# Reordering the last block of a convolution and MLP kernel: output products with the raw activations last, one of them by token halves

## The chip, the cores and the metric

The kernel runs on one core of one Trainium2 chip. The metric is the device time of one execution in microseconds (us), the median of several. A run counts as slow when it lies more than 1.5% above the fastest of the same kernel.

The span of the profile is about 1.7 us shorter than the time of the same execution.

The **tail** runs from the first matmul of the last block's output products to the end of the span, and a **tail time** counts from that same matmul.

## The reference, cut to what matters

```
x (8, 4096, 192), weight (8 heads, 7 taps), w_in (192, 2048), w_out (2048, 192), all float32

w   = softmax of weight over the taps
out = causal 7-tap convolution of x over the sequence, one set of taps per head of 24 channels
h   = out.reshape(32768, 192) @ w_in
g   = h * (1 / (1 + exp(-h)))          # silu
y   = g @ w_out                        # (32768, 192), what is stored
```

## The kernel before: the parts that matter here

The 32768 tokens are worked in 32 blocks of 1024. A block is first multiplied by `w_in` ("up") into `g`, then by `w_out` ("down"). Both products of a block use a scheme with seven products of halves of the matrices instead of eight. In "down" the halves are two token groups of 512 and two channel halves of 96, so the result has four slices: C11, C12, C21, C22, held as `c[0]` to `c[3]`.

The seven products lie in six accumulator banks (`acc[0]` to `acc[5]`, called slots 0 to 5). They are summed over four steps `j`. A slot holds a product of 96 rows, and in its last 32 rows a piece of another. Slots 0 and 1 multiply the raw `g`. Slots 2 to 5 need sums of `g` that VectorE makes first (`t`).

```
# the order of work, one token per step: t = a sum of g, z/y/x = ScalarE copies out of the
# accumulators, M = VectorE adds of the slots, o = turn and store a slice; "-" = of the block before
PLAN = (
    "P1.0 P1.1 -x1.0 -M4.0 | P1.2 P5.0 -M5.0 s1.1 -M7.0 | P5.1 E22.0 s1.0 -o.1 s1.2 | "
    "E22.1 P6.1 -o.2 | P6.0 P1.3 s2.1 | P6.2 P5.2 -o.3 s1.3 s2.0 | P5.3 P7.1 s2.2 | "
    # ... cut ...
    "t.30 | . | t.31 | w.0 | t.32 | . | t.33 | . | w.1 | w.2 | z1.0 w.3 | y0.0 | y1.0 | "
    ". | y2.0 M1.0 | M2.0 | M6.0 | x0.0 | M3.0 x2.0 | o.0"
)

def down(b, j):
    # ... cut: a_, forms: which product takes which weights and which of g and t ...
    sets = ((1, 2, 0), (3, 2, 1), (6, 2, 2), (7, 4, 0), (5, 4, 1))
    for i in (0, 1, 2, 4, 3, 5) if j < NJ - 1 else (0, 1, 2, 3, 5, 4):
        if j == 0:
            accs[b][i] = bank()
        for e in range(2):
            # ... four matmuls into the quarters of slot i, mm(i, q, every, lhs, q, rhs, e) ...
            yield

def merge(b, name):
    # ... cut: the copies x, y, z on ScalarE; the last of them is
    pin(nc.scalar.copy(to, acc[3 * (name[0] == "x") + k][n:P, :]))
    # ... and the adds on VectorE
    out_, u, v = {
        "M1": lambda: (c[1], c[0], acc[2][0:n, :]),
        "M2": lambda: (c[3], c[1], acc[1][0:n, :]),
        "M3": lambda: (c[2], c[1], acc[3][0:n, :]),
        "M4": lambda: (c[1], c[3], acc[4][0:n, :]),
        "M5": lambda: (c[3], c[2], acc[4][0:n, :]),
        "M6": lambda: (c[0], c[0], t["y"][0:n, :]),
        "M7": lambda: (c[2], c[2], t["x"][0:n, :]),
    }[name]()

def turn_out(b, i):
    # 32x32 transposes of slice i on VectorE, then one store per 32 channels
    pin(nc.vector.transpose(osb[0:top, i, :, :]..., cmbs[b][0][0:top, i, :]))
    for q in range(top // SQ):
        queue = (nc.sync, nc.scalar, nc.gpsimd)[q % 3] if b == NB - 1 else nc.sync
        queue.dma_start(out=out_v[2 * b + n][:, :, c : c + SQ], in_=osb[...])

for b in range(1, NB):
    run(b, plan[:NU])
    begin_down(b)
    slots = (None for j in range(NJ) for _ in down(b, j))
    for s in plan[NU:]:
        next(slots)
        run(b, [s])
run(NB, plan[:NU])           # what is left of the last block: x1 M4 M5 M7 o.1 o.2 o.3
```

In an inner block, the merges and the stores of the block before lie beside the next block's matmuls. Only the last block has no next one: its last copy, adds, transposes and stores lie open.

Of the kernel before, what the change touches and what calls it, by code (L numbers as in the profile page):

```python
# [9 lines left out]
F32 = mybir.dt.float32  # L10
I32 = mybir.dt.int32
AF = mybir.ActivationFunctionType
ALU = mybir.AluOpType
# [4 lines left out]
def kernel(  # L18
# [24 lines left out]
    nc = tc.nc  # L43
# [6 lines left out]
    P = 128  # L50
# [4 lines left out]
    TB = 512  # L55
    TT = 2 * TB
    NB = NT // TT
    NCH = DFF // P
    NM = NCH // 2
    NJ = NM // 2  # L60
    SQ = 32
    HD = D // 2
    NP = HD // SQ
# [3 lines left out]
    out_v = out.rearrange("(n k t) d -> n t k d", k=TB // SQ, t=SQ)  # L67

    const = ctx.enter_context(tc.tile_pool(name="const", bufs=1))
    xpool = ctx.enter_context(tc.tile_pool(name="xp", bufs=1))  # L70
    tpool = ctx.enter_context(tc.tile_pool(name="tp", bufs=3))
    gpool = ctx.enter_context(tc.tile_pool(name="gp", bufs=2 * NJ))
    upool = ctx.enter_context(tc.tile_pool(name="up", bufs=13))
# [29 lines left out]
    def pin(ins):  # L103
        return tc.keep_in_program_order(ins)
# [8 lines left out]
    vec = Pinned(nc.vector)  # L113

    def bank():
        return psum.tile([P, TB], F32, tag="ps", name="ps")
# [3 lines left out]
    def load(b):  # L120
# [12 lines left out]
        out=wexp.rearrange("p h k -> p (h k)"),  # L133
        in_=weight.rearrange("(o h) k -> o (h k)", o=1).to_broadcast([P, H * K]),
# [5 lines left out]
    for k in range(NK):  # L140
        nc.gpsimd.dma_start(
            out=xts[0][R:P, k, 0:pad], in_=x0[:, k, :], allow_slow_non_contiguous=True
# [116 lines left out]
    for e in range(2):  # L259
        half = hot[R * e : R * e + R]  # L260
        for sign, base in ((1, 0), (-1, grp - 1)):
            nc.gpsimd.affine_select(
                out=half,
                in_=half,
# [20 lines left out]
    for k in range(NK):  # L285
# [4 lines left out]
            op=ALU.mult,  # L290
# [96 lines left out]
    bk, us, sums, cmbs, accs = {}, {}, {}, {}, {}  # L387

    def product(b, m, name):
        d, t = dups[b], wins[b]  # L390
        e, r, s = m % 2, wr[m // 2], ws[m // 2]

        other, bn, w, v = {
            "P1": (0, "1", r[:, 0, 0, :], d[:, 0, 0, :]),
            "P6": (0, "1", r[:, 0, 1, :], t[:, 1, :]),
            "P7": (0, "1", r[:, 1, 0, :], t[:, 2, :]),
            "P4": (0, "1", r[:, 1, 1, :], t[:, 3, :]),
            "E21": (0, "1", r[:, 1, 2, :], d[:, 0, 2, :]),
            "P2": (1, "b", s[:, 0, 1, :], d[:, 0, 1, :]),
            "E11": (1, "b", s[:, 0, 2, :], d[:, 0, 2, :]),  # L400
            "P5": (1, "d", s[:, 1, 0, :], t[:, 0, :]),
            "E22": (1, "d", s[:, 1, 2, :], d[:, 1, 2, :]),
            "P3": (1, "d", s[:, 0, 0, :], d[:, 1, 1, :]),
            "E12": (1, "d", s[:, 1, 1, :], d[:, 1, 2, :]),
        }[name]
        half = e ^ other
        first = (b, m, bn) not in bk
        if first:
            bk[b, m, bn] = bank()
        pin(  # L410
            nc.tensor.matmul(  # L411
                bk[b, m, bn], rows(w, half), rows(v, half), start=first, stop=True,
                skip_group_check=True,
            )
        )
# [4 lines left out]
    def sums_h(b, name, m):  # L420


        if name[0] == "s":
            u = us[b, m, name[1]] = upool.tile([P, TB], F32, tag="u", name="u")
            copy = nc.vector.tensor_copy if name == "s2" else nc.scalar.copy
            pin(copy(u, bk[b, m, "1"]))  # L426
            return
        g = g_of(b, m, int(name[1]) - 1, int(name[2]) - 1)
        if name == "C21":
            pin(nc.scalar.activation(g, bk[b, m, "1"], AF.Silu))  # L430
        elif name[0] == "g":
            pin(nc.scalar.activation(g, g, AF.Silu))  # L432
        else:
            i, bn = {"C11": ("1", "b"), "C22": ("3", "d"), "C12": ("2", "d")}[name]
            pin(nc.vector.tensor_tensor(g, us.pop((b, m, i)), bk[b, m, bn], op=ALU.add))  # L435
# [15 lines left out]
        )[i]()  # L451
        pin(nc.vector.tensor_tensor(t[i // 2][:, i % 2, :], u, v, op=ALU.subtract))  # L452

    def down(b, j):



        if j == 0:
            accs[b] = {}
        g = [gs[b, j, a] for a in range(2)]  # L460
        w, x_ = wo[j], wx[j]

        def t(i):
            return sums[b, j][i // 2][:, i % 2, :].rearrange("p (e t) -> p e t", e=2)

        def mm(i, q, cols, lhs, c, rhs, e):
            pin(
                nc.tensor.matmul(  # L468
                    accs[b][i][SQ * q : SQ * q + SQ, cols],
                    lhs[:, e, SQ * c : SQ * c + SQ],  # L470
                    rhs[:, e, cols] if i < 5 else rhs[:, e, ts(q, TB // 4)],
                    start=j == 0 and e == 0,
                    stop=j == NJ - 1 and e == 1,
                    skip_group_check=True,
                )
            )

        a_ = [[w[:, a, :, HD * u : HD * u + HD] for a in range(2)] for u in range(2)]
        forms = {
            1: lambda: (a_[0][0], g[0][:, 0]),  # L480
            2: lambda: (a_[0][1], g[1][:, 0]),
            3: lambda: (x_[:, 2], g[1][:, 1]),
            4: lambda: (a_[1][1], t(3)),
            5: lambda: (x_[:, 0], t(0)),
            6: lambda: (x_[:, 1], t(1)),
            7: lambda: (a_[1][0], t(2)),
        }
        sets = ((1, 2, 0), (3, 2, 1), (6, 2, 2), (7, 4, 0), (5, 4, 1))
        every = slice(0, TB)

        for i in (0, 1, 2, 4, 3, 5) if j < NJ - 1 else (0, 1, 2, 3, 5, 4):
            if j == 0:
                accs[b][i] = bank()
            for e in range(2):
                if i < 5:
                    own, other, c = sets[i]
                    for q in range(NP):
                        lhs, rhs = forms[own]()
                        mm(i, q, every, lhs, q, rhs, e)
                    lhs, rhs = forms[other]()  # L500
                    mm(i, NP, every, lhs, c, rhs, e)
                else:
                    lhs, rhs = forms[4]()
                    for q in range(4):
                        mm(5, q, slice(0, TB // 4), lhs, 2, rhs, e)
                yield
        for a in range(2):
            del gs[b, j, a]
# [63 lines left out]
    osbs = {}  # L572

    def turn_out(b, i):
        if b not in osbs:
            osbs[b] = tpool.tile([P, 4, TB // SQ, SQ], F32, tag="t", name="osb")
        osb = osbs[b]
        top = HD if b else P
        pin(
            nc.vector.transpose(  # L580
                osb[0:top, i, :, :].rearrange("p k c -> p (k c)"), cmbs[b][0][0:top, i, :]
            )
        )
        for q in range(top // SQ):
            n, c = (i % 2, HD * (i // 2) + SQ * q) if b else (q // 2, R * i + SQ * (q % 2))
            queue = (nc.sync, nc.scalar, nc.gpsimd)[q % 3] if b == NB - 1 else nc.sync
            queue.dma_start(  # L587
                out=out_v[2 * b + n][:, :, c : c + SQ], in_=osb[SQ * q : SQ * q + SQ, i, :, :]
            )

    plan = [slot.split() for slot in PLAN.split("|")]
    NU = NM * 11 // 2
    did = set()

    def step(b, token):

        if token[0] == "-":
            b, token = b - 1, token[1:]
        name, arg = token.split(".") if "." in token else ("", "")
        if b < 0 or b >= NB or not name or (b, token) in did:  # L600
            return
        did.add((b, token))
        digits = [int(c) for c in arg]
        if name[0] in "PE":
            product(b, digits[0], name)
        elif name[0] in "sCg":
            if b:
                sums_h(b, name, digits[0])
        elif name == "t":
            sum_g(b, *digits)  # L610
        elif name[0] in "Mzyx":
            merge(b, name)
        elif name == "o":
            turn_out(b, *digits)
        elif b + 1 < NB:
            {"i": turn_in, "v": conv, "w": win}[name](b + 1, *digits)
            if name == "v" and digits[1] == K - 1 and (b, "down") in did:
                spread(b + 1, digits[0])
                if digits[0] == NK - 1 and b + 2 < NB:
                    load(b + 2)  # L620
# [7 lines left out]
    def run(b, slots):  # L628
        for s in slots:
            for token in s:  # L630
                step(b, token)


    for k in range(NK):
        turn_in(0, k)
# [33 lines left out]
    for k in range(NK):  # L669
        turn_out(0, k)  # L670
# [3 lines left out]
    for b in range(1, NB):  # L674
        run(b, plan[:NU])
        begin_down(b)
        slots = (None for j in range(NJ) for _ in down(b, j))
        for s in plan[NU:]:
            next(slots)
            run(b, [s])  # L680
        assert next(slots, 0) == 0
    run(NB, plan[:NU])


# [28 lines left out]
```

## Time and profile before

| | before |
|---|---|
| median of three runs | 2429.41 us (2428.07 to 2429.82) |
| profiled span | 2428.0 us |
| first output product of the last block | 2381.26 us |
| last matmul ends, tail time | 36.29 us |
| last transpose ends, tail time | 41.31 us |
| last store has landed, tail time | 45.23 us |
| span ends, tail time | 46.75 us |

How the views are read: PE is TensorE, DVE VectorE, ACT ScalarE, POOL GpSimd, SP SyncE. `L468` is a line of the kernel and `x2` a count. `ACTq` is a store issued from ScalarE's queue. The chain of waits is followed back from the last instruction, and each of its lines is a start, a duration and what ran. In the timeline, the bracket gives the idle time before an instruction and who ended it. In the view of transfers, the last two columns are the size of one transfer and the median time from issue to landing. The lines themselves stand in the prediction below.

### The profile page before, as it was taken

What the parts mean: (1) busy time and instruction counts of PE and PEld (TensorE: products, weight loads), DVE (VectorE), ACT (ScalarE), POOL (GpSimd) and SP (SyncE); (2) the same over time, 40 slices, a digit from 0 to 9 for tenths busy, and PEclk for the clock granted to TensorE, in tenths of its full rate; (3) what the DMA queues carried; (4) which work ended last, traced back from release to release, by engine and by line L of the source; (5) the groups of instructions that cost most, each with busy time, mean ns of one, the idle gap of its engine ahead of it and who ended that gap; (6) DMA issues with size and microseconds to landing.
All of it is one profiled execution on the core that took longest, in us unless ns stands there. A gap on an engine that the chain in (4) does not pass through costs nothing.

```text
span 2428.0 us, 42997 instructions
## 1 busy us (share of the span) xinstructions
PE 2391.3 (98%) x17744; PEld 939.2 (39%) x17744; DVE 2075.0 (85%) x2810; ACT 980.8 (40%) x1840; POOL 62.0 (3%) x92
## 2 busy tenths in 40 slices
PE   5999999999999999999999999999999999999998
PEld 3334433344333344333443333443334433334432
DVE  8898888898888988888988889888889888898875
ACT  2145433345333454333453334543334533345432
POOL 2300000000000000000000000000000000000000
PEclk9999999999999999999999999999999999999999
DMA  7321222212222222222122222122221222222210
GB/s 153 75 44 35 36 53 53 40 38 38 45 53 43 42 39 36 53 53 40 38 38 44 53 44 46 35 36 53 53 40 38 37 45 53 43 43 39 36 40 14
DMA packets 452260, 111.64 MB, mean 46 GB/s; under 512 B 421792, under 2 KB 426912, under 8 KB 452064
## 3 DMA queue, kind: packets, MB, share of 16 engines
q1 hardware_dynamic: 447056, 105.84, 22.6%
q10 hardware_dynamic: 4784, 2.78, 0.6%
q8 instruction: 139, 2.28, 0.4%
q14 instruction: 57, 0.47, 0.1%
q0 software_dynamic: 224, 0.27, 0.0%
HBM read 31.49 MB, written 25.17 MB: 23 GB/s over the span
## 4 chain that ended last, share of the span: by engine, by line
PE 98%; DVE 1%; DMA 1%; ACT 0%; issue 0%; ACTq 0%; POOL 0%; SPq 0%; POOLq 0%; DVEq 0%
PE ps L411 48%; PE ps L468 46%; PE ps L519 2%; PE ps L375 1%; DMA nat<-in_x_dram 0%; DVE nat L325 0%; DVE two L111 0%; DMA raw<-in_moe_w_in_dram 0%; DVE cmb L570 0%; DVE mh L111 0%; DVE xt L305 0%; POOL out_dram L587 0%; SPq L165 0%; ACT L385 0%; DVE osb L580 0%
## 5 line engine op out<-in xcount | busy, mean ns | idle before, releaser
L411 PE MATMUL ps<-dup,ws 64*128 64x512 f32 x2480 | 869.9, 589 | 0.0
L468 PE MATMUL ps<-g,wo 128*32 128x512 f32 x2976 | 662.0, 593 | 0.0
L435 DVE TENSOR_TENSOR g<-u,ps 128x512 f32<-128x512 f32 x744 | 485.8, 680 | 119.1 <-PE ps L411 89.8
L411 PE MATMUL ps<-win,wr 64*128 64x512 f32 x1488 | 567.7, 589 | 0.0
L468 PE MATMUL ps<-t,wo 128*32 128x512 f32 (+1 forms) x4464 | 500.7, 450 | 0.0
L432 ACT ACTIVATE g<-g 128x512 f32<-128x512 f32 x744 | 444.7, 631 | 97.4 <-DVE g L435 97.4
L411 PEld LDWEIGHTS ps<-dup,ws 64*128 64x128 f32 x2480 | 363.0, 187 | 292.0 <-issue 277.9
L468 PE MATMUL ps<-t,wx 128*32 128x512 f32 x2976 | 453.1, 592 | 0.0
L325 DVE SCALAR_TENSOR_TENSOR nat<-xt,taps,nat 128x512 f32<-128x512 f32 x576 | 432.2, 750 | 15.1
L411 PE MATMUL ps<-dup,wr 64*128 64x512 f32 x992 | 419.9, 596 | 0.0
L426 ACT COPY u<-ps 128x512 f32<-128x512 f32 x496 | 277.7, 588 | 229.1 <-PE ps L411 226.1
L558 ACT COPY cmb<-ps 96x512 f32<-96x512 f32 x31 | 18.0, 581 | 832.1 <-PE ps L468 832.1
L452 DVE TENSOR_TENSOR t<-g 128x1024 f32<-128x1024 f32 x248 | 299.8, 1220 | 27.0 <-PE ps L468 27.0
L452 DVE TENSOR_TENSOR t<-g,t 128x1024 f32<-128x1024 f32 x248 | 303.4, 1224 | 17.9 <-PE ps L468 7.4
L411 PEld LDWEIGHTS ps<-win,wr 64*128 64x128 f32 x1488 | 233.4, 187 | 175.5 <-issue 147.2
L468 PEld LDWEIGHTS ps<-t,wo 128*32 128x32 f32 x4464 | 178.3, 110 | 222.6 <-issue 204.9
L411 PE MATMUL ps<-win,ws 64*128 64x512 f32 x496 | 242.2, 589 | 0.0
L468 PE MATMUL ps<-g,wx 128*32 128x512 f32 x1488 | 234.7, 592 | 0.0
L468 PEld LDWEIGHTS ps<-t,wx 128*32 128x32 f32 x2976 | 121.9, 110 | 278.2 <-issue 268.7
L570 DVE TENSOR_TENSOR cmb<-cmb,ps 96x512 f32<-96x512 f32 x155 | 105.7, 682 | 141.9 <-ACT u L555 139.7
L411 PEld LDWEIGHTS ps<-dup,wr 64*128 64x128 f32 x992 | 160.5, 187 | 128.2 <-issue 114.3
L468 PEld LDWEIGHTS ps<-g,wo 128*32 128x32 f32 x2976 | 168.5, 110 | 97.7 <-issue 97.7
(53 smaller groups left out, 1191.3 us busy)
## 6 DMA issues: line engine op xcount, KB each, us to landing
dup<-nat SPq DMA_DIRECT2D x384, 128.0 KB, 2.3
nat<-in_x_dram SPq DMA_DIRECT2D x382, 64.0 KB, 2.4
out_dram<-osb SPq DMA_DIRECT2D x376, 64.0 KB, 1.9
raw<-in_moe_w_out_dram SPq DMA_DIRECT2D x8, 384.0 KB, 3.5
raw<-in_moe_w_in_dram SPq DMA_DIRECT2D x12, 192.0 KB, 4.2
ws<-wr ACTq DMA_DIRECT2D x8, 192.0 KB, 5.6
raw<-in_moe_w_in_dram ACTq DMA_DIRECT2D x4, 192.0 KB, 5.9
xt<-xt SPq DMA_DIRECT2D x31, 4.5 KB, 1.9
```

Of the source, the lines that this page charges most:

```text
L325: nc.vector.scalar_tensor_tensor(out=dst, in0=src, scalar=tap, in1=dst, op0=ALU.mult, op1=ALU.add)
L375: nc.tensor.matmul(hs[a, n, e], rows(wr[j], e)[:, a, k, :], rows(d, e)[:, n, k, :], start=k == 0, stop=k == NK - 1,)
L411: nc.tensor.matmul(bk[b, m, bn], rows(w, half), rows(v, half), start=first, stop=True, skip_group_check=True,)
L426: pin(copy(u, bk[b, m, "1"]))
L432: pin(nc.scalar.activation(g, g, AF.Silu))
L435: pin(nc.vector.tensor_tensor(g, us.pop((b, m, i)), bk[b, m, bn], op=ALU.add))
L452: pin(nc.vector.tensor_tensor(t[i // 2][:, i % 2, :], u, v, op=ALU.subtract))
L468: nc.tensor.matmul(accs[b][i][SQ * q : SQ * q + SQ, cols], lhs[:, e, SQ * c : SQ * c + SQ], rhs[:, e, cols] if i < 5 else rhs[:, e, ts(q, ...
L519: nc.tensor.matmul(acc[k][R * n : R * n + R, :], wo[j][:, a, e, R * k : R * k + R], gs[b, j, a][:, n, e, :], start=j == 0 and a == 0 and e ...
L558: pin(nc.scalar.copy(c[0], acc[0][0:n, :]))
L570: pin(nc.vector.tensor_tensor(out_, u, v, op=ALU.add))
```

## The change

The change concerns the last block alone. In its last two steps `j`, the four slots that need sums come first, so that the adds of C21 and C22 are nearly complete when slot 0 is. Slot 0 comes next, and slot 1 last. C22 and C21 never need slot 1, so they can be summed, turned and stored while slot 1's matmuls still run. Slot 1 is done in two halves of 256 tokens, so that the first half could be merged and stored during the second half's matmuls.

```diff
-    def down(b, j):
+    def out_slot(b, j, i, e, half=None):      # one slot of one step, all tokens or a half
 ...
+            to = slice(0, TB // 4) if i == 5 else slice(0, TB) if half is None else ts(half, TB // 2)
+            pin(nc.tensor.matmul(accs[b][i][SQ * q : SQ * q + SQ, to], lhs..., rhs...[to], ...))
 ...
+    def finish(b):
+        late = (NJ - 2, NJ - 1)
+        for j in late:
+            for k in (0, 1, 3, 2):
+                step(b, f"t.{j}{k}")
+            for i in (2, 4, 3, 5):
+                for e in range(2):
+                    out_slot(b, j, i, e)
 ...     # copies and adds of slots 2 to 5 into c[1], c[2], c[3]
+        for j in late:
+            for e in range(2):
+                out_slot(b, j, 0, e)
+        for half in range(2):
+            for j in late:
+                for e in range(2):
+                    out_slot(b, j, 1, e, half)
+            if half:
+                break
+            pin(nc.scalar.copy(c[0], acc[0][0:n, :]))
+            pin(nc.scalar.copy(part(y, 0), acc[0][n:P, :]))
+            add(c[3], c[3], acc[0][0:n, :])
+            store(3, every)                    # transpose, then SyncE, ScalarE, GpSimd store 32 channels each
+            add(c[2], c[2], acc[0][0:n, :])
+            store(2, every)
+            add(c[1], c[1], acc[0][0:n, :])
+        for half in range(2):
+            cols = slice(half * TB // 2, (half + 1) * TB // 2)
+            pin(nc.scalar.copy(part(y, 1)[:, cols], acc[1][n:P, cols]))
+            add(c[1][:, cols], c[1][:, cols], acc[1][0:n, cols])
+            store(1, cols)
+            add(c[0][:, cols], c[0][:, cols], y[0:n, cols])
+            store(0, cols)
 ...
-        slots = (None for j in range(NJ) for _ in down(b, j))
+        slots = (None for j in range(NJ // 2 if last else NJ) for _ in down(b, j))
 ...
-    run(NB, plan[:NU])
+    finish(NB - 1)
```

More of the change, by code (lines that the diff above doesn't have):

```diff
@@ L452, in sum_g, with t @@
         pin(nc.vector.tensor_tensor(t[i // 2][:, i % 2, :], u, v, op=ALU.subtract))
-    def down(b, j):
-        if j == 0:
-            accs[b] = {}
+    def out_slot(b, j, i, e, half=None):
         g = [gs[b, j, a] for a in range(2)]
         w, x_ = wo[j], wx[j]
-        def t(i):
-            return sums[b, j][i // 2][:, i % 2, :].rearrange("p (e t) -> p e t", e=2)
-        def mm(i, q, cols, lhs, c, rhs, e):
-            pin(
-                nc.tensor.matmul(
-                    accs[b][i][SQ * q : SQ * q + SQ, cols],
-                    lhs[:, e, SQ * c : SQ * c + SQ],
-                    rhs[:, e, cols] if i < 5 else rhs[:, e, ts(q, TB // 4)],
-                    start=j == 0 and e == 0,
-                    stop=j == NJ - 1 and e == 1,
-                    skip_group_check=True,
-                )
-            )
+        if i not in accs.setdefault(b, {}):
+            accs[b][i] = bank()
+        def t(k):
+            return sums[b, j][k // 2][:, k % 2, :].rearrange("p (e t) -> p e t", e=2)
         a_ = [[w[:, a, :, HD * u : HD * u + HD] for a in range(2)] for u in range(2)]
@@ L487, in down @@
         }
-        sets = ((1, 2, 0), (3, 2, 1), (6, 2, 2), (7, 4, 0), (5, 4, 1))
-        every = slice(0, TB)
+        own, other, c = ((1, 2, 0), (3, 2, 1), (6, 2, 2), (7, 4, 0), (5, 4, 1), (4, 4, 2))[i]
+        for q in range(4):
+            lhs, rhs = forms[own if q < NP else other]()
+            k = c if i == 5 or q == NP else q
+            to = slice(0, TB // 4) if i == 5 else slice(0, TB) if half is None else ts(half, TB // 2)
+            pin(
+                nc.tensor.matmul(
+                    accs[b][i][SQ * q : SQ * q + SQ, to],
+                    lhs[:, e, SQ * k : SQ * k + SQ],
+                    rhs[:, e, ts(q, TB // 4) if i == 5 else to],
+                    start=j == 0 and e == 0,
+                    stop=j == NJ - 1 and e == 1,
+                    skip_group_check=True,
+                )
+            )
+    def down(b, j):
         for i in (0, 1, 2, 4, 3, 5) if j < NJ - 1 else (0, 1, 2, 3, 5, 4):
-            if j == 0:
-                accs[b][i] = bank()
             for e in range(2):
-                if i < 5:
-                    own, other, c = sets[i]
-                    for q in range(NP):
-                        lhs, rhs = forms[own]()
-                        mm(i, q, every, lhs, q, rhs, e)
-                    lhs, rhs = forms[other]()
-                    mm(i, NP, every, lhs, c, rhs, e)
-                else:
-                    lhs, rhs = forms[4]()
-                    for q in range(4):
-                        mm(5, q, slice(0, TB // 4), lhs, 2, rhs, e)
+                out_slot(b, j, i, e)
                 yield
@@ L585, in turn_out @@
             n, c = (i % 2, HD * (i // 2) + SQ * q) if b else (q // 2, R * i + SQ * (q % 2))
-            queue = (nc.sync, nc.scalar, nc.gpsimd)[q % 3] if b == NB - 1 else nc.sync
-            queue.dma_start(
+            nc.sync.dma_start(
                 out=out_v[2 * b + n][:, :, c : c + SQ], in_=osb[SQ * q : SQ * q + SQ, i, :, :]
@@ L631, in run, with part, add, store @@
                 step(b, token)
+    def finish(b):
[5 more added lines that the diff above has]
+                for e in range(2):
+                    out_slot(b, j, i, e)
+        acc, n = accs[b], HD
+        cmb = xpool.tile([P, 4, TB], F32, tag="cmb", name="cmb")
+        cmbs[b] = [cmb]
+        c = [cmb[0:n, i, :] for i in range(4)]
+        y, x_ = (upool.tile([P, TB], F32, tag="u", name="u") for _ in range(2))
+        def part(t, k):
+            return t[SQ * k : SQ * k + SQ, :]
+        def add(out_, u, v):
+            vec.tensor_tensor(out_, u, v, op=ALU.add)
+        def store(i, cols, rows_=slice(0, n)):
+            if b not in osbs:
+                osbs[b] = tpool.tile([P, 4, TB // SQ, SQ], F32, tag="t", name="osb")
+            osb = osbs[b][:, i, :, :].rearrange("p k c -> p (k c)")
+            vec.transpose(osb[rows_, cols], cmb[rows_, i, cols])
+            ks = slice(cols.start // SQ, cols.stop // SQ)
+            for q in range(rows_.start // SQ, rows_.stop // SQ):
+                ch = HD * (i // 2) + SQ * q
+                (nc.sync, nc.scalar, nc.gpsimd)[q % 3].dma_start(
+                    out=out_v[2 * b + i % 2][:, ks, ch : ch + SQ],
+                    in_=osbs[b][SQ * q : SQ * q + SQ, i, ks, :],
+                )
+        every = slice(0, TB)
+        pin(nc.scalar.copy(c[1], acc[2][0:n, :]))
+        pin(nc.scalar.copy(part(y, 2), acc[2][n:P, :]))
+        pin(nc.scalar.copy(part(x_, 1), acc[4][n:P, :]))
+        add(c[2], c[1], acc[3][0:n, :])
+        pin(nc.scalar.copy(part(x_, 0), acc[3][n:P, :]))
+        add(c[3], c[2], acc[4][0:n, :])
+        add(c[1], c[1], acc[4][0:n, :])
+        for q in range(4):
+            pin(
+                nc.scalar.copy(
+                    part(x_, 2)[:, ts(q, TB // 4)], acc[5][SQ * q : SQ * q + SQ, 0 : TB // 4]
+                )
+            )
+        add(c[2], c[2], x_[0:n, :])
+        for j in late:
[21 more added lines that the diff above has]
+            store(0, cols)
@@ L676 @@
         begin_down(b)
-        slots = (None for j in range(NJ) for _ in down(b, j))
-        for s in plan[NU:]:
-            next(slots)
+        last = b == NB - 1
+        if last:
+            did.update((b, t.lstrip("-")) for s in plan for t in s if t.lstrip("-")[0] in "Mzyxo")
+        slots = (None for j in range(NJ // 2 if last else NJ) for _ in down(b, j))
+        for s, _ in zip(plan[NU:], slots):
             run(b, [s])
         assert next(slots, 0) == 0
-    run(NB, plan[:NU])
+    finish(NB - 1)
 _INS = ['x', 'weight', 'moe_w_in', 'moe_w_out']
```

## The prediction

> **What bounds the kernel now.** I read the page first, then the chain of waits at its end, then the timeline and the stores of the last 25 us.
>
> ```profile
> PE 2391.3 (98%) x17744; PEld 939.2 (39%) x17744; DVE 2075.0 (85%) x2810; ACT 980.8 (40%) x1840; POOL 62.0 (3%) x92
> DVE  8898888898888988888988889888889888898875
> PE ps L411 48%; PE ps L468 46%; PE ps L519 2%; PE ps L375 1%; DMA nat<-in_x_dram 0%; DVE nat L325 0%; DVE two L111 0%; DMA raw<-in_moe_w_in_dram 0%; DVE cmb L570 0%; DVE mh L111 0%; DVE xt L305 0%; POOL out_dram L587 0%; SPq L165 0%; ACT L385 0%; DVE osb L580 0%
> ```
>
> TensorE is busy 98% of 2428.0 us and carries the chain. In the chain by time its pieces are seamless from 43 to 2413.7 us: 37.97 us of up products (L411), then 36.22 us of output products (L468), thirty-one times. The change leaves all blocks but the last alone: without line numbers, the order of instructions is the same on every engine up to there. So only what follows the last matmul can shrink.
>
> The chain of the last microseconds (start, length, what):
>
> ```profile
> 2416.95 0.63 DVE osb L580
> 2417.59 0.02 issue
> 2417.61 0.38 ACTq L587
> 2417.99 0.04 issue
> 2418.03 0.59 ACT u L555
> 2418.62 0.02 issue
> 2418.64 0.69 DVE cmb L570
> ...
> 2420.76 0.63 DVE osb L580
> 2421.40 0.28 issue
> 2421.68 1.29 POOL out_dram L587 x2
> 2422.97 0.64 POOLq L708
> ```
>
> The last group of matmuls (four at a time) starts at 2416.93 and takes 0.61. Then come: a store issue on ScalarE that stands ahead of its last copy, that copy, three adds, three transposes, nine stores. The DMA view of short windows (2421.4 to 2421.7, then from 2422.8; the last number is us from issue to landing):
>
> ```profile
> out_dram<-osb POOLq DMA_DIRECT2D x1, 64.0 KB, 2.9
> ...
> out_dram<-osb POOLq DMA_DIRECT2D x2, 64.0 KB, 3.5
> out_dram<-osb SPq DMA_DIRECT2D x1, 64.0 KB, 2.9
> ```
>
> and the timeline, with in brackets the idle time before and who ended it:
>
> ```profile
> 2418.64 1.40 DVE L570 TENSOR_TENSOR cmb<-cmb,ps 96x512 f32<-96x512 f32 x2 [1.06 <-ACT u L555]
> 2420.68 1.89 DVE L580 STREAM_TRANSPOSE osb<-cmb 96x512 f32<-96x512 f32 x3
> 2421.68 1.93 POOL L587 DMA_DIRECT2D out_dram<-osb  x3 [3.14 <-DVE osb L580]
> ```
>
> GpSimd's three stores follow each other; the last starts at 2422.97 and lands 3.5 later, at 2426.48. The first semaphore step of the closing code on SyncE (its event semaphores) is recorded at 2426.50 and the span ends at 2428.0. So 10.4 us lie between the last matmul's end (2417.54) and the end: 0.5 behind the store issue, 4.5 of copy, adds and transposes, 3.9 until the last store has landed, 1.5 of closing code.
>
> **What the Trainium skill says.** (1) "PSUM — Partial Sum Buffer", section on bank collisions: two engines must not touch one bank in the same 32-partition quadrant at once, reads against reads included, and guards go by bank and quadrant, not by address. The trace agrees in form: VectorE's add of slot 3 starts at 2418.64, 0.02 after ScalarE's copy out of the same bank, having waited 1.06. In the program built from the changed kernel, ScalarE's copy of the first token half waits for TensorE count 8888, the last matmul of both halves (first half alone: 8872). (2) The same page, "Engine vs sequencer instructions": ScalarE's queue is strict FIFO. The trace agrees: its last copy waits for a store issued 2417.61 to 2417.99. (3) "DMA: Bandwidth & Descriptors", section "Issuing engines are not separate DMA queues": stores of all engines share 16 DMA engines. Agrees: SyncE's landing grows from 2.0 to 2.9, ScalarE's from 2.2 to 3.6 within the burst of nine. (4) "Perfetto Trace Analysis", SWDGE section: GpSimd's issue ends when descriptors are generated, before the data moves. Agrees: 0.65 us issued, 2.7 to 3.5 to landing.
>
> **The change, part by part.**
> *Matmuls.* Blocks j=0,1 stay. For j=2,3 the four slots that need sums come first, then slot 0, then slot 1 in halves of 256 tokens. A group of four takes 0.429 us per pass at 512 columns, two passes, two e: 1.716 us a slot; slot 5 (128 columns) 0.445, from 9.02 us a block. The halves make 16 groups of 0.214 for 8 of 0.429: the same 3.43. Weight loads double there, but four take 0.13 and hide, and slot 5's even narrower groups cost about 0.02 extra. So the stream still ends at about 2417.6. Will TensorE wait for sums? Block j=2 starts at 2399.32 and needs sums finished by 2393.1 and 2399.8; j=3 starts at 2404.91, its first sum ready at 2402.2 and its last at about 2405.4 (the t buffer is freed by slots 2 and 4 of j=2, 2402.8, then two sums of 1.2), wanted at 2406.6. No wait. New completion times: slots 2, 4, 3, 5 by 2410.5; slot 0's last group starts at 2413.50.
> *ScalarE before the end.* A copy has started 0.67 us after the start of its slot's last group; slot 0's copies start at 2414.17, take 0.59 + 0.58, and VectorE's first add waits for both: 2415.37.
> *VectorE.* Pitches in the trace: 0.72 after a dependent, 0.60 after an independent instruction of 512 columns. From durations (512: 0.68; 1024: 1.22) 256 columns save 0.27: 0.45 and 0.34. From 2415.37: add c3, transpose 2416.09, add c2 2416.69, transpose 2417.41, add c1 2418.01, free at 2418.73. Two of the four output slices are now turned and stored before TensorE's tail is drained; that is the gain intended.
> *The halves.* ScalarE's second store waits for the transpose that ends at 2418.14, is issued in 0.42, and only then the first half's copy runs: 2418.56 (TensorE's end, 2417.6, is not what it waits for). VectorE: add 2418.96, transpose 2419.41, add 2419.75, transpose 2420.20. ScalarE now has two stores ahead of the second half's copy, the later waiting until 2420.67: copy at 2421.09. VectorE idles 0.9 us and goes on: 2421.48, 2421.93, 2422.27, last transpose 2422.72, done 2423.19. That is 0.6 **later** than the last transpose of before (2422.57).
> *Stores.* Two slices leave early (issued 2416.8 and 2418.1). At the end there are six stores of 32 KB in two bursts of three instead of nine of 64 KB in one. GpSimd starts 0.27 after SyncE: 2423.45. An uncrowded 64 KB store of its landed in 2.7; half as large I estimate 2.4 (from the 2.0 to 2.9 above): 2425.85, against 2426.48.
> *Closing code.* Before, the last store was the first semaphore that SyncE waited for; after it came nine steps of 0.06. Now the last one stands seventh, so some 0.36 of these pass before it lands: end = landing + 1.14 instead of + 1.50. Span 2427.0: **1.0 us less.**
>
> **Rivals.**
> (a) *The halves pipeline as meant*: the first half's copy runs beside the second half's matmuls. It could then start at 2416 rather than 2418.56 if nothing stood ahead in ScalarE's queue, but VectorE isn't free before 2418.73: worth at most 0.2 more. Against it: the count 8888.
> (b) *VectorE/ScalarE interleaving eats everything*: if GpSimd's small stores land no faster than 2.9, the end is 2427.5, a gain of 0.5; if they queue, zero. For it: the end of the transposes moves later; the fixed part of a landing is large.
> (c) *TensorE stalls* on t buffers or on the doubled weight loads: each missed sum costs up to 1.2 us, and the kernel gets 0.5 to 1.5 us slower. Against: margins of 1.2 us or more at every sum.
> (d) *Everything hidden as intended* (stores of the halves alone after the matmuls, end of matmuls + 5 us of copy, adds, transposes, store and closing): 2425, a gain of 3. Against: the ScalarE queue order above.
>
> **Range and chances.** The trace was 2428.0 for a run of 2429.71; the three timed runs spread 1.75 us (2428.07 to 2429.82), more than the effect. Median before 2429.41 less 1.0: 2428.4. With rivals (d) and (b)/(c) and the spread, 2426.8 to 2429.8. All of the tail after the last matmul is 0.43% of the time, so 2% (48.6 us) is out of reach either way: same 0.985; faster 0.01; slower 0.005 for something that I overlooked.
>
> **What would show it.** Right: matmuls of the last block without a gap and ending near 2417.6; the first half-copy of slot 1 starting behind a ScalarE store at about 2418.6; VectorE idle about 0.9 us before the second half's add, ended by ScalarE; the last transpose ending near 2423.2, later than before; last GpSimd store landing near 2425.9; span near 2427. Wrong: a gap in TensorE before block j=3's slots; the first half's copy starting before the last matmul ends; landings of small stores above 3 us. It would be wrong altogether if the earlier blocks moved, by another placement of buffers or a throttled clock (0.998 here).

## The result

| | before | changed |
|---|---|---|
| median | 2429.5 us (6 runs) | 2427.56 us (6 runs) |
| range | 2428.07 to 2430.69 | 2426.97 to 2428.45 |
| profiled span | 2428.0 | 2425.3 |
| granted clock of the profiled run | 0.998 | 0.998 |

The ratio is 0.9992, with a 95% interval of 0.998 to 1.0005: the same, at 2%. A ratio here is the mean time of one kernel's fast runs over the mean of the other's of the same rounds, so it is not quite the ratio of the medians quoted. The medians differ by 1.94 us, more than the end of the kernel accounts for, as the views below show.

The busy times of the page of the changed kernel:

```profile
PE 2389.4 (99%) x17776; PEld 939.1 (39%) x17776; DVE 2077.2 (86%) x2816; ACT 981.4 (40%) x1842; POOL 62.6 (3%) x94
```

The kernel is still TensorE's. It has 32 more matmul records from the halves, and 6 more VectorE, 2 more ScalarE and 2 more GpSimd instructions.

The chain of waits of the changed kernel, its last microseconds:

```profile
2413.29 0.59 ACT u L684
2413.90 0.69 DVE cmb L111
2414.62 0.71 DVE osb L111
...
2416.67 0.37 ACTq L654
2417.05 0.04 issue
2417.09 0.38 ACT u L692
...
2419.19 0.38 ACTq L654
2419.57 0.04 issue
2419.61 0.38 ACT u L692
...
2420.91 0.28 issue
2421.19 0.58 POOL out_dram L654
```

Before, the chain held one store on ScalarE's queue (`ACTq`) ahead of a copy. Now it holds two: the first ahead of the copy of the first half, the second ahead of the copy of the second half. The last matmul ends at 2416.06, so neither copy waits for TensorE any more. VectorE's timeline shows the price:

```profile
2420.01 0.42 DVE L111 TENSOR_TENSOR cmb<-cmb,ps 96x256 f32<-96x256 f32 x1 [0.85 <-ACT u L692]
...
2421.24 0.44 DVE L111 STREAM_TRANSPOSE osb<-cmb 96x256 f32<-96x256 f32 x1
```

VectorE idles 0.85 us before the second half's first add and waits for that ScalarE copy. The first output product of the last block starts at 2379.75, so the last transpose ends at tail time 41.93. That is 0.62 **later** than before. What saves the change is the stores, in the view of transfers of the last 10 us:

```profile
out_dram<-osb POOLq DMA_DIRECT2D x2, 64.0 KB, 2.5
out_dram<-osb SPq DMA_DIRECT2D x4, 32.0 KB, 1.6
out_dram<-osb ACTq DMA_DIRECT2D x4, 32.0 KB, 1.7
out_dram<-osb POOLq DMA_DIRECT2D x4, 32.0 KB, 1.9
```

Before, GpSimd's last stores of 64 KB took 3.5 us in a burst of nine. Now its last ones, of 32 KB in bursts of three, take 1.9. The last store lands at tail time 44.10 against 45.23, and the tail is 45.52 against 46.75 us: **1.23 us less**.

That is not the whole difference between these two profiled runs. The spans differ by 2.7, of which 1.5 lies before the tail: the first output product of the last block starts at 2381.26 before and at 2379.75 now, although nothing was changed ahead of it. The table of stretches at the start of the program shows where this comes from. The columns are the stretch in us, its length, TensorE's busy time with the matmuls, then the granted clock as a share of the full one, the share of the transfer engines and GB/s. Before:

```profile
43.00:46.00 3.00, 2.88 (x7) 0.61 1.10 211
46.00:50.00 4.00, 4.00 (x18) 0.87 0.99 273
```

Changed:

```profile
43.00:46.00 3.00, 2.89 (x13) 1.00 1.12 212
46.00:50.00 4.00, 4.00 (x21) 1.00 0.97 250
```

Before, a stretch at half clock, from 43.66 to 47.07 in the clock record, fell on the first dense matmuls: 23 of them ran in these 7 us instead of 31 (one window of 43 to 50). In the run of the changed kernel it fell earlier, from 35.84 to 39.26, when TensorE had little to do. So I set out to test two things: whether the 1.5 us belong to the change, and which part of the change makes the 1.23 us of the tail.

### The profile page after: what moved, and what is told of

Same layout as the page of the kernel before. It is cut to its first block, busy times and chain, and to the rows that moved or that the text cites. A ratio compares the mean times of both kernels' runs of the same rounds, so it can differ in the third digit from the quotient of the medians.

```text
span 2425.3 us, 43085 instructions
## 1 busy us (share of the span) xinstructions
PE 2389.4 (99%) x17776; PEld 939.1 (39%) x17776; DVE 2077.2 (86%) x2816; ACT 981.4 (40%) x1842; POOL 62.6 (3%) x94
## 4 chain that ended last, share of the span: by engine, by line
PE 98%; DVE 1%; DMA 0%; issue 0%; ACT 0%; ACTq 0%; POOLq 0%; POOL 0%; DVEq 0%
PE ps L411 49%; PE ps L482 46%; PE ps L510 2%; PE ps L375 1%; DVE nat L325 0%; DVE two L111 0%; DMA raw<-in_moe_w_in_dram 0%; DMA wexp<-in_weight_dram 0%; DVE mh L111 0%; DVE osb L111 0%; DVE cmb L111 0%; DVE xt L305 0%; DVE nat L322 0%; ACT L385 0%; ACTq L219 0%
## 5 line engine op out<-in xcount | busy, mean ns | idle before, releaser
L482 PE MATMUL ps<-g,wx 128*32 128x512 f32 (+1 forms) x1512 | 234.6, 585 | 0.0
```

The costliest lines, as they stand in the source:

```text
L482: nc.tensor.matmul(accs[b][i][SQ * q : SQ * q + SQ, to], lhs[:, e, SQ * k : SQ * k + SQ], rhs[:, e, ts(q, TB // 4) if i == 5 else to], sta ...
```

## The experiments

All kernels gave correct results. They ran each on one chip and beside runs of the kernel before. The theory: the tail's gain comes from storing two slices early, the halves cost more than they give because of the order on ScalarE's queue, and the difference ahead of the tail is chance. The rivals: the halves give the gain; the shared accumulator bank holds the halves back; the changed program itself moves the start-up.

### Both kernels again

No edit: the kernel before and the changed kernel, on another chip.

> The kernel before, unchanged. Tail = time from the first output product of the last block to the end of the span. Theory (the change acts on the tail alone; the rest of the difference of the two traces is the phase of the half-clock window at the start): tail 46.75 +-0.15 as in the first trace, whatever the span is; the spans of the runs spread over 1 to 2 us, and the start of the last block's output products moves with the place of the half-clock window (2381.3 when it lies on the first matmuls, 2379.8 when it lies before them). Rival (the change also made the earlier blocks 1.5 us faster): the last block's output products start at 2381.3 again in every profile of this kernel.

> The changed kernel, unchanged. Theory: tail 45.52 +-0.15 in this trace too; the start of the last block's output products is 2379.8 or 2381.3 depending on the half-clock window, so some runs have spans 1 to 1.5 us over the shortest. Rival: the start is 2379.8 every time because the earlier blocks are faster.

Measured: tails of 46.76 and 45.51 us, as in the first traces. The medians were 2429.89 and 2427.4, the ratios to the kernel before 1.0001 (0.9987 to 1.0016) and 0.9992 (0.9975 to 1.0008). In these two profiles the start-up was the other way round. The chain of waits of the kernel before:

```profile
2379.61 4.41 PE ps L468 x37
```

and of the changed kernel:

```profile
2381.21 3.12 PE ps L482 x25
```

The output products of the last block began early in the kernel **before** and late in the **changed** one. The half-clock stretch ended at 34.62 in the former and lay at 44.63 to 48.04 in the latter. What follows: the tail is a property of the kernel, and the 1.5 us ahead of it also appear in one and the same kernel.

### The two early stores moved to the end

```diff
             add(c[3], c[3], acc[0][0:n, :])
-            store(3, every)
             add(c[2], c[2], acc[0][0:n, :])
-            store(2, every)
             add(c[1], c[1], acc[0][0:n, :])
 ...
             store(0, cols)
+        store(3, every)
+        store(2, every)
```

> As the changed kernel, but the two slices that are ready early are turned and stored after everything else. If storing them meanwhile is what the gain comes from, VectorE's last transpose ends about where it did (1.3 us of transposes moved behind, but also taken out from before) and six full stores queue at the end: last landing 1 to 1.5 us later, tail 46.5 to 47.0, the gain gone. If the gain comes from the order of the products alone, tail stays 45.5 +-0.2.

Measured: tail 47.01 us, 1.5 more than the changed kernel and 0.3 more than before. The median was 2430.49, the ratio 1.0004 (0.9989 to 1.0019). The end of its chain of waits, then the transfers of the last stretch:

```profile
2422.53 0.58 POOL out_dram L654
2423.11 0.20 issue
2423.31 0.58 POOL out_dram L654
2423.90 0.01 issue
2423.91 0.65 POOL out_dram L654
2424.55 0.64 POOLq L775
```

```profile
out_dram<-osb SPq DMA_DIRECT2D x2, 64.0 KB, 2.4
out_dram<-osb ACTq DMA_DIRECT2D x2, 64.0 KB, 2.9
out_dram<-osb POOLq DMA_DIRECT2D x2, 64.0 KB, 3.1
```

The transposes end only 0.22 later than in the changed kernel (tail time 42.15 against 41.93). The last stores are large and crowded again: GpSimd issues them one behind another, and its last takes 3.1 us to land instead of 1.9. What follows: the whole gain of the change hangs on the two slices being gone before the end. The last GpSimd store is issued 0.26 later (42.49 against 42.23) and lands 1.24 slower (3.11 against 1.87), which makes the 1.5.

### Slot 1 whole, no halves

```diff
-        for half in range(2):
-            for j in late:
-                for e in range(2):
-                    out_slot(b, j, 1, e, half)
-            if half:
-                break
+        for j in late:
+            for e in range(2):
+                out_slot(b, j, 1, e)
 ...
-        for half in range(2):
-            cols = slice(half * TB // 2, (half + 1) * TB // 2)
-            ...  # copy, add, store, add, store of a half
+        pin(nc.scalar.copy(part(y, 1), acc[1][n:P, :]))
+        add(c[1], c[1], acc[1][0:n, :])
+        store(1, every)
+        add(c[0], c[0], y[0:n, :])
+        store(0, every)
```

> As the changed kernel, but slot 1 is not cut into token halves (512 columns in matmuls, copy, adds, transposes, stores). If the halves pay as intended, tail grows by 0.5 or more (46.0 to 46.6). My theory: the halves cost as much as they give, because both wait for the last matmul anyway and ScalarE's stores of the first half delay the copy of the second: without them VectorE ends 1.2 us earlier (last transpose at 40.7 in tail time instead of 41.93), but the last stores are of 64 KB and land 0.6 later than small ones: tail 44.9 to 45.3, 0.2 to 0.6 less than the changed kernel.

Measured: tail 44.90, median 2427.51, ratio 0.9992 (0.9977 to 1.0007). The last transpose ends at tail time 40.69, where 40.70 was expected. VectorE's timeline:

```profile
2418.88 0.68 DVE L111 TENSOR_TENSOR cmb<-cmb,ps 96x512 f32<-96x512 f32 x1 [0.49 <-ACT u L688]
```

One idle time of 0.49 is left, and no second one of 0.85. The reason in the expectation, that both halves wait for the last matmul, is not what the changed kernel shows: its first half waits for a store. What follows: as written, the halves cost 0.62 us of tail. Each smaller store lands faster after its issue, but the second half waits for the queue.

### Both copies of slot 1 ahead of the stores

```diff
-        for half in range(2):
-            cols = slice(half * TB // 2, (half + 1) * TB // 2)
+        halves = [slice(half * TB // 2, (half + 1) * TB // 2) for half in range(2)]
+        for cols in halves:
             pin(nc.scalar.copy(part(y, 1)[:, cols], acc[1][n:P, cols]))
+        for cols in halves:
             add(c[1][:, cols], c[1][:, cols], acc[1][0:n, cols])
```

> As the changed kernel, but ScalarE copies both halves of slot 1 before it issues any store of them. Theory (in ScalarE's queue, stores that wait for transposes stand ahead of the second half's copy and cost VectorE 0.85 us of idling): that idle time goes; VectorE's first half add starts 0.4 later, since it waits for both copies, so its last transpose ends 0.5 to 0.6 earlier (41.35 in tail time, 41.93 in the changed kernel) and tail is 44.9 to 45.1. Rival (the wait is for something else, TensorE or VectorE's own chain): tail 45.5 +-0.1.

Measured: tail 44.80, a little under the range expected, last transpose 41.25, median 2427.25, ratio 0.9991 (0.9978 to 1.0005). ScalarE's timeline:

```profile
2418.20 0.64 ACT L692 COPY u<-ps 32x256 f32<-32x256 f32 x2 [3.22 <-DVE osb L111]
2419.79 2.72 ACTq L654 DMA_DIRECT2D out_dram<-osb  x4
```

The two copies run back to back, and all four stores come after them. What follows: moving one copy ahead of two stores on the same queue is worth 0.7 us of tail. That is most of VectorE's idle time of 0.85. The first copy still waits 3.22 us, until the last of the two large transposes lets the store ahead of it go. With the second wait gone, the kernel with halves is within 0.1 us of the one with slot 1 whole (44.80 against 44.90).

### The second half in a bank of its own

```diff
-        if i not in accs.setdefault(b, {}):
-            accs[b][i] = bank()
+        key = 6 if half else i
+        if key not in accs.setdefault(b, {}):
+            accs[b][key] = bank()
 ...     # steps j = 0, 1 of slot 1 of the last block go by halves too; copies and adds read their half's bank
```

> As the changed kernel, but in the last block the second half of slot 1 is summed in a bank of its own, so the first half's copy no longer waits for the second half's matmuls. Theory: that wait for the whole bank isn't what ends last, ScalarE's store is; tail unchanged, 45.5 +-0.15. Rival (the shared bank takes away the overlap that the halves were meant to give): first half copy 0.9 us earlier and tail 0.4 to 0.9 less. A stall of TensorE for the seventh bank would show as a later last matmul (36.3 in tail time).

Measured: tail 45.48, against 45.52 and 45.51 of the changed kernel, so nothing. The last matmul ends at 36.33, against 36.31. The median was 2428.11, the ratio 0.9996 (0.9982 to 1.0009). ScalarE's timeline:

```profile
2418.26 0.37 ACT L697 COPY u<-ps 32x256 f32<-32x256 f32 x1 [3.22 <-DVE osb L111]
```

The copy no longer needs the second half's matmuls, and it starts where it did (tail time 37.37 against 37.34) because the store is ahead of it. What follows: the wait for both halves was real in the program, but it was not the last to end. The rival with the bank falls for this order of the queue. Whether the bank would matter with a mended queue was not run.

### VectorE's adds ahead of ScalarE's copies, early stores off ScalarE

Here the adds of slot 0 no longer wait for ScalarE. The stores of the first two slices go to SyncE and GpSimd, the copies of both halves come ahead of all ScalarE stores, and VectorE adds both halves before it turns them.

```diff
+            for i in (3, 2, 1):
+                add(c[i], c[i], acc[0][0:n, :])
             pin(nc.scalar.copy(c[0], acc[0][0:n, :]))
             pin(nc.scalar.copy(part(y, 0), acc[0][n:P, :]))
-            add(c[3], c[3], acc[0][0:n, :])
-            store(3, every)
-            add(c[2], c[2], acc[0][0:n, :])
-            store(2, every)
-            add(c[1], c[1], acc[0][0:n, :])
+            turn(3, every)
+            turn(2, every)
+            send(3, every, (nc.sync, nc.sync, nc.gpsimd))
+            send(2, every, (nc.sync, nc.sync, nc.gpsimd))
 ...
+        for cols in halves:
+            add(c[1][:, cols], c[1][:, cols], acc[1][0:n, cols])
+        for cols in halves:
+            pin(nc.scalar.copy(part(y, 1)[:, cols], acc[1][n:P, cols]))
 ...     # then turn c[1] by halves, send it, and add, turn, send c[0] by halves
```

> From what the runs showed: VectorE reads slot 0's and slot 1's banks before ScalarE does, ScalarE makes all copies before any store of the last four, the early slices go out by SyncE and GpSimd. VectorE's three adds of slot 0 start at 32.97 in tail time instead of 34.15, slot 1's adds at 36.4 right behind the last matmul instead of 37.7 and 40.3; last transpose ends at 39.5, last GpSimd store (32 KB, 1.87) lands at 41.65, tail 43.1 (42.8 to 43.4), 2.4 less than the changed kernel, 3.7 less than before. If instead the landing or the closing code bounds the tail, it stays above 44.5.

Measured: tail 43.06 us, 2.45 less than the changed kernel and 3.7 less than before. The median was 2425.56, the ratio to before 0.9985 (0.9972 to 0.9999), so it beats both kernels in the median. VectorE's timeline:

```profile
2412.78 1.88 DVE L111 TENSOR_TENSOR cmb<-cmb,ps 96x512 f32<-96x512 f32 x3 [0.71 <-PE ps L482]
2414.59 1.29 DVE L111 STREAM_TRANSPOSE osb<-cmb 96x512 f32<-96x512 f32 x2
2416.24 0.75 DVE L111 TENSOR_TENSOR cmb<-cmb,ps 96x256 f32<-96x256 f32 x2 [0.36 <-PE ps L482]
```

Both idle times in these lines are now ended by TensorE (`PE ps`) and none by ScalarE: the adds of slot 1 start 0.07 after the last matmul ends (2416.17). A new wait appeared. SyncE's waits in the last stretch (us in total, times, longest):

```profile
SPq L655 <- DMA out_dram<-osb: 1.3, 2, 1.1
```

SyncE's last two stores are issued at tail times 39.73 and 40.13, while ScalarE's of the same two slices left at 38.62 and 39.40. The first of the two waits for the semaphore of an earlier transfer: ScalarE's store of 37.51 uses the same one and lands at 39.66. The second stands behind it in SyncE's queue. They land at 41.65 and 42.06, and the last GpSimd store at 41.86, so SyncE's is now the last. This kernel changes several things at once (adds ahead of copies, both halves added before either is turned, copies ahead of stores, other queues for the early stores). Only the copies ahead of stores were run alone, so how the 2.45 us divide is not shown.

### The same with slot 1 whole

The edit is that of the kernel just above together with that of "slot 1 whole, no halves".

> As vector_first, but slot 1 uncut (no token halves). Last transpose ends at 39.2, 0.3 earlier, but the last stores are of 64 KB and land in 2.4: 41.9; closing 1.5: tail 43.4 (43.1 to 43.7), within 0.4 of vector_first. If halves pay once the queue order is mended, vector_first is the shorter by 0.3; if they still cost, vector_whole is.

Measured: tail 43.57, median 2426.17, ratio 0.9987 (0.9975 to 1.0). The last transpose ends earlier than with halves (39.11 against 39.37), and the last store lands earlier too (41.75 against 42.06). Yet the tail is 0.5 longer, because 1.8 us pass from that landing to the end of the span instead of 1.0. The traces show where the 0.8 us of difference lie. With slot 1 whole, SyncE goes through nine waits after the last landing, with halves through two, since the store that lands last stands at another place in its order. That is some 0.45. SyncE also stands still for 0.34 us, from 42.35 to 42.69, where no landing is left to wait for. With halves a gap of 0.35 (41.58 to 41.93) lies before the last landing. Why SyncE stands still is not known. What follows: with the queue mended the halves no longer cost tail, but the 0.5 that they gain comes from the closing code. They do not bring the last landing forward.

### Both kernels a third time

No edit, five rounds on another chip, for the start-up.

> The changed kernel once more. Time less 1.70 (what the time has over the span) less the tail (45.52; 46.75 before) gives for each run the start of the last block's output products. If the 0.5 to 0.7 us by which the changed kernel's runs gained more than its tail did are chance in the phase of the half-clock windows, its mean start comes nearer to that of before (2380.9 in the runs so far) than the 2380.3 of its runs so far. If it is a property of the program, its mean start stays at 2380.3 +-0.2.

> The kernel before once more, for the same comparison: tail 46.75 +-0.1, mean start 2380.9 +-0.3.

Measured: medians 2427.88 (0.9993, 0.998 to 1.0007) and 2429.51 (1.0003, 0.999 to 1.0015). By luck the half-clock stretch fell at the same place in both profiles, 43.25 to 46.67 and 43.30 to 46.71. The tables of stretches, of the changed kernel and of the kernel before:

```profile
43.00:46.00 3.00, 2.95 (x7) 0.54 1.13 210
```

```profile
43.00:46.00 3.00, 3.00 (x7) 0.55 1.12 213
```

The last block's output products then start at 2381.03 and 2381.02. The spans are 2426.5 and 2427.8, the tails 45.47 and 46.79. What follows: with the start-up equal, the whole difference of 1.3 us is the tail.

**The start-up over all runs.** Nearly every run lists its span. If I take off the tail of its kernel, as its profiles show it, what is left is where the last block's output products began. The first six runs of the kernel before have no span and are left out, as is its first profiled one. These starts come in three levels, near 2379.7, 2380.9 and 2382.1 us:

| runs | near 2379.7 | near 2380.9 | near 2382.1 or above | mean |
|---|---|---|---|---|
| kernel before, 34 | 6 | 23 | 5 | 2380.89 |
| changed kernel, 15 | 7 | 8 | 0 | 2380.43 |
| its six variants above, 26 | 7 | 15 | 4 | 2380.84 |

The changed kernel's 15 runs began 0.46 earlier on average than those of the kernel before, with a standard error of 0.20. The expectation of the third trial was that more runs would decide whether this is a property of the program. Its five new starts had a mean of 2380.5, between the two values expected, so that trial alone is inconclusive. The six variants speak for chance, though. They were made from the changed kernel by edits in the code of its last block alone, and their mean is 0.05 from that of the kernel before. All 41 runs of this family have a mean of 2380.69, which is 0.2 below the kernel before, with a standard error of 0.18 for the difference. Pooling them was decided after the runs. I count the 0.46 as not shown to belong to the change; it is not ruled out either.

### All tails together

| kernel | last transpose ends | last store landed | tail |
|---|---|---|---|
| before | 41.31 | 45.23 | 46.75 |
| changed | 41.93 | 44.10 | 45.52 |
| early stores moved to the end | 42.15 | 45.60 | 47.01 |
| slot 1 whole | 40.69 | 43.37 | 44.90 |
| copies ahead of stores | 41.25 | 43.40 | 44.80 |
| second half in its own bank | 41.95 | 44.11 | 45.48 |
| adds first, early stores off ScalarE | 39.37 | 42.06 | 43.06 |
| the same, slot 1 whole | 39.11 | 41.75 | 43.57 |

## Why the prediction was right

The time predicted was 2428.4 in a range of 2426.8 to 2429.8, and the median measured is 2427.56. The mechanism was right, with two terms mis-sized. The number owes something to luck: of the 1.94 us between the two medians, 1.23 are the tail, and the other 0.7 lie in the start-up, which the prediction did not foresee.

- **The bound and the matmuls.** No wait for sums or weights appeared: the last matmul ends at tail time 36.31 against 36.29 before. Rival (c), a stall of TensorE, did not occur.
- **VectorE and ScalarE.** On the tail's clock, the first add of slot 0 was put at 34.11 and came at 34.15. The copy of the first half was put at 37.30, behind a ScalarE store, and came at 37.34. VectorE's idle time before the second half was put at 0.9 (0.8 by the prediction's own times) and was 0.85. The last transpose was put at 41.93 and ended at 41.93.
- **Landing of the last store: mis-sized.** The prediction put 2.4 us for a 32 KB store of GpSimd, and it took 1.87. The estimate scaled too little with size: an uncrowded 64 KB store took 2.5 in the same trace. This gave 0.5 more gain than predicted.
- **Closing code: mis-sized the other way.** Predicted 1.14 us after the last landing, measured 1.42. One step on SyncE took 0.38 where the prediction counted steps of 0.06. SyncE stands still there, from 44.19 to 44.54 in tail time. In the kernel before it stood still for 0.38, from 46.05 to 46.43, while GpSimd was still clearing semaphores (until 46.42), so it cost little there. Why it stands still, and why at another place in another program, stays open. The same stretch took 1.0 to 1.8 in the other kernels.
- **The sum.** 42.23 (issue of the last GpSimd store, 42.19 predicted) + 1.87 + 1.42 = 45.52, against 45.74 predicted. So the tail shrank by 1.23 where 1.0 was predicted.
- **What the prediction did not see.** It took the start of the last block's outputs as fixed. Between the first two traces that start moved by 1.5 us, more than the tail did. The spread in its range covered this.
- **The rivals.** (a), the bank, was worth nothing as the queue stands. (b), small stores landing no faster than 2.9, was wrong by 1 us. (d), a gain of 3, did not come with this order of the queues; the variant with adds and copies put ahead and the early stores on other queues shrank the tail by 3.7. The sum in (d) does not come out as written: 2417.6 + 5 is 2422.6, not 2425. In that variant 6.75 us lie between the last matmul's end and the end of the span.
- **A reading that was wrong.** In point (1) of what the prediction takes from the skill, the add at 2418.64 reads slot 4, not slot 3. It reads rows 0 to 95, and the copy that it waited for reads rows 96 to 127, so they lie in different quadrants. The wait of 1.06 us therefore shows that this program keeps the engines apart by the whole bank; it does not show the rule by quadrant. Whether the two could have run together was not tried.

So where did the intended gain go? With slot 1 whole, the new order gains 1.85 us (46.75 to 44.90), and the halves as written take 0.62 back, which leaves 1.23. Without the early stores the changed kernel is 1.5 longer, so no gain is left. Putting both copies ahead of the stores wins back 0.7: that is the loss by the halves undone, and not a further cost. The best variant is 2.45 shorter than the changed kernel. This includes the order of copies and stores, and the shares of its other edits were not measured.

## What to carry to other kernels

When work is split so that its parts overlap, look at the in-order queue of every engine that carries both stores and compute. A store that waits for another engine holds back every later copy on that queue (here VectorE idled for 0.85 us), and the split can then cost more than it gives. At the end of a kernel, look at when the last store lands: send finished slices early, so that few stores crowd at the end. Smaller stores alone did not help here: in the two pairs of kernels without the second wait, the last landing was no earlier with halves (43.40 against 43.37, and 42.06 against 41.75). The closing code after it can differ by 0.8 us between programs, so read it separately. When an effect is smaller than the spread of the runs, measure it from an event that starts after the noisy part, and compare two runs of one and the same kernel before explaining any difference.

## What the Trainium skill lacked or had wrong

- "DMA: Bandwidth & Descriptors", section on the anatomy of one DMA (SWDGE path), gives about 2.0 us plus bytes over 436 GB/s. By an estimate from that formula, half of a 64 KB store saves 0.08 us. Here GpSimd's stores took 2.4 to 2.7 at 64 KB when little else was stored, and 1.83 to 1.95 at 32 KB: a saving of about 0.4 to 0.9, and a 32 KB store lies below the fixed part. Nearly all packets of these stores are under 512 bytes (4384 of 4481 in the last stretch). That this is the reason was not tested.
- No page has what crowding adds to small stores. A 64 KB store of GpSimd took up to 3.6 us in a burst of nine. 32 KB stores took 1.55 (SyncE), 1.75 (ScalarE) and 1.87 (GpSimd) in bursts of three, and 1.92 to 2.37, 2.05 to 2.62 and 2.19 to 2.47 when 12 of them followed within 2.7 us.
- "PSUM — Partial Sum Buffer", section "Engine vs sequencer instructions", says that ScalarE's queue is strict FIFO, and the traces agree. It does not say that a store issued from it, waiting for another engine, therefore holds later compute. Here that cost 0.85 us of VectorE's time, and putting the copy ahead gave 0.7.
- "TensorE: Matmul & The Clock Gate", Part 1, has a free-running window of 3413 ns and calls the penalty of the ramp under 1%. This agrees: half-clock stretches of 3.41 us, one of 6.8, move the time by 1.2 to 2.5 us, or 0.05 to 0.1%. The page says that the ramp varies from run to run, but not that this can be larger than what a change at the end of a kernel is worth, nor that the starts fall into levels some 1.2 us apart, as they do here.
- No page has the closing code of the kernel's own program, apart from what the runtime puts around it: 1.0 to 1.8 us from the last landing to the end of the span here, with a standstill of SyncE of 0.34 to 0.38 in it in eleven of the twelve traces.
